# Windowed attention with one expert per sentence on one Trainium2 core: 64-column pooled sums for batch 0, and a new order of all steps

## The chip, the core and the metric

The kernel runs on one core of a Trainium2 chip. The core has TensorE (matrix products into PSUM), VectorE, ScalarE and GpSimd, and SyncE, which here issues stores. DMA engines move data between HBM and the core's memory, SBUF. GpSimd issues all loads, on one queue. The metric is the device time of one execution in microseconds (us), the median of several runs.

## The reference

The input is q, k and v for 8 batches ("sentences"), 8 heads, 576 positions and a head dimension of 64. Each head attends within a window of 32 positions on either side. The result, 576 x 512 for each batch, goes through one of 8 experts, chosen for the whole sentence from the mean over its positions:

```python
scores = scale * np.matmul(q, k.transpose(0, 1, 3, 2))
mask = np.abs(pos[:, None] - pos[None, :]) <= 32
attn = softmax(np.where(mask, scores, -1e9))          # per head
x = np.matmul(attn, v)                                # then B, S, H*D
pooled = x.mean(axis=1)                               # 8 x 512
logits = pooled @ w_gate                              # 8 x 8
e_idx = np.argmax(logits, axis=1)                     # one expert per batch
out[mask] = gate_w[mask, None, None] * (np.maximum(x[mask] @ w1[e], 0.0) @ w2[e])
```

The weights of an expert, 512 x 1024 and 1024 x 512, can be loaded only when the batch's pooled sums have chosen it.

## The kernel before

Each batch goes through the same steps, and each step has a short name with the batch number in it. For batch b:

- `ldqb`, `ldkb`, `ldvb` (L286, L314) load q, k and v, cast to 16 bits. `Tqb0`, `Tqb1` and so on (L300, L327) transpose them on VectorE.
- `Sb0` to `Sb2` (L417) are the score products on TensorE, `Xb..` (L440) the exponentials on ScalarE. In batches 0 and 1 a fill `ZSb.` (L397) first writes the window's mask into PSUM; in the others `Mb.` (L450) multiplies the mask in on VectorE.
- `Vb0`, `Vb1` (L347) turn v on TensorE, `Cb0`, `Cb1` (L360 on ScalarE, L362 on VectorE) copy it into the tile va, and `Db..` (L373 on ScalarE or VectorE, L375 on GpSimd) make its copies shifted by 64 positions, 64 x 528 numbers each.
- `Ab0` to `Ab2` (`Ab4` in batch 0) (L469) are the attention products, 28 + 28 + 16 of them in batch 1; `NAb.` (L541, L542) divides by the softmax sums on VectorE and so frees the PSUM pair.
- `Rb0`, `Rb1` (L571, L574) turn the result on TensorE, `CRb..` (L586 on VectorE, L588 on ScalarE in batch 0, L590 otherwise) copy it out as xT.
- `Lb` (L650, L655) makes the logits, `Gb` (L667, L668) finds the expert, `GNb` and `GXb` its exponentials, `W1b` and `W2b` (L695 and L719 for batch 0, L704 and L724 otherwise) load its weights. Batch 0's first weights come in three pieces, `W10`, `WB1` and `WB2`.
- `1b0` to `1b7` (L753) are the first expert products, eight matrix products each, `R1b.` their ReLU (L768, L770). `2b...` (L833, L796) are the second ones, `E2b...` scale and copy them out (L781, L784), and `O2b...` store them (L861, L814).

In batch 0 the pooled sums are made on TensorE itself, by the steps `pool0` to `pool4` (L616): each product has 64 columns of a unit of 128 rows of attention output as its stationary operand (the loaded weights), and as its moving operand one column, either ones (`pick`, parts 0 and 1, fp16) or the reciprocals of the softmax sums (`linv`, parts 2 to 4, fp32, which use the undivided output copied by `U02` to `U04`, L518 and L520, with the reciprocals from `I02` to `I04`, L507). Even and odd heads use the two column halves of the array. `pcopy` (L629) copies the 128 x 4 sums out of PSUM. In later batches the sums come with the copies CR, for nothing.

The order of the work is written out by hand in the string `ORDER`: one list of step names, with the engine behind a colon where there is a choice. `Plan.finish` (L109) goes through it and emits each step; each engine then runs its own steps strictly in that order, and waits where an operand isn't ready. GpSimd's list holds the loads, the shifted copies D, the pads and the broadcasts GB. Buffers are handed out in the same pass: PSUM is four pairs of banks, and a step that takes a pair gets the one that was freed first, so it waits for the step that freed it. In front of some TensorE steps `busy` (L234) issues products of a constant tile (`KEEP`), whose output is overwritten.

The order around the change, from the table: in the old order A10 comes after `100`, `wg` (the gate matrix of the later batches) ahead of `W10`, and `ldk4` ahead of `W12`.

Of the kernel before, what the change touches and what calls it, by code (L numbers as in the profile page):

```python
# [10 lines left out]
FP32 = mybir.dt.float32  # L11
# [13 lines left out]
P = 128  # L25
# [15 lines left out]
}  # L41

ORDER = """
ldq00 ldk00 ldv00 ldv01 ldk01 ldq01 cu0 ldk1 wg0 cp1 ldq1 cp0 ldv1 ldk2 ca cb Tq00 Tk00 ZS00 S00
X001 Tv00 V00 Tv01 X000 C00:DVE D001:ACT ZS01 V01 Tk01 D000:ACT Tq01 A00 C01:ACT D011:ACT D010:SW
wg ldq2 A01 cu1 NA00 NA01 S01 X011 X010 ZS02 S02 A03 A02 X021 X020 Tk10 Tk11 I03 U03:ACT A04 pool0
I02 U02:DVE I04 U04:ACT NA02 Tq10 Tq11 pool1 pool2 pool3 pool4 pcopy:ACT L0 G0 GN0 GX0 W10 NA03
Tv10 Tv11 ZS10 S10 X101 X100 ZS11 S11 WB1 WB2 V10 V11 Tk20 NA04 X110 Tk21 C10:ACT C11:DVE X111 R00
ldv2 CR000:ACT R01 CR001:ACT W20 CR010:DVE D101:SW CR011:DVE D100:SW ZS12 S12 100 Tq20 D110:SW Tq21
D111:SW X120 X121 A10 R100:ACT ldv3 NA10 A12 NA12 101 102 R101:ACT A11 R102:ACT S20 103 X201 NA11  # L50
R10 X200 R103:DVE Tv20 GW0 Tv21 R11 CR100 CR110 CR101 104 R104:ACT CR111 LP1 105 R105:ACT 106 ldk3
R106:DVE S21 X210 107 X211 R107:DVE L1 G1 GN1 W11 V20 C20:ACT V21 C21:ACT M21 M20 D201 GX1 D200
20000 Tv30 Tv31 20001 20010 S22 GW1 D210 X221 X220 20011 20100 D211 20101 M22 A20 A21 ldq3 20110
W21 20111 GB1 GB0 NA20 NA21 20t A22 E2000:ACT E2010:ACT V30 V31 NA22 E20t:ACT C30:ACT C31:DVE D310
D311 ldv4 Tk30 D300 Tk31 D301 R20 Tq30 CR200 R21 110 CR210 CR211 CR201 LP2 111 R110:ACT 112
R111:ACT 113 R113:ACT R112:DVE L2 G2 GN2 GX2 114 115 R114:ACT R115:ACT Tq31 S30 X301 X300 116 117
R116:ACT 21000 R117:ACT S31 X310 X311 M31 21001 21010 M30 Tv40 S32 X321 21011 21100 X320 Tv41
E2100:ACT 21101 21110 V40 21111 C40:ACT A30 M32 21t A31 ldq4 ldk4 E2110:ACT GW2 Tq40 A32 NA30 V41
E21t:ACT W12 W22 NA32 120 121 R120:ACT NA31 R30 R121:ACT C41:DVE D401 CR300 CR301 ldv5 O21t O2110
Tk40 D411 Tk41 D400 R31 Tq41 122 123 124 R122:ACT 125 CR310 CR311 R124:ACT R123:ACT ldq5 LP3 L3 G3  # L60
W13 GN3 D410 GB2 R125:ACT GX3 126 Tv50 S40 R126:ACT X401 127 22000 X400 S41 R127:DVE X411 X410
22001 22010 S42 X420 X421 Tv51 M40 Tq50 Tq51 ldk5 M41 22011 22100 E2200:DVE 22101 22110 22111 W23
A40 M42 O2000 E2210:ACT A42 22t NA40 NA42 E22t:ACT O22t ldv6 O2200 A41 130 NA41 V50 O2010 GW3 131
C50:ACT R130:DVE 132 R132:DVE R131:ACT Tk50 Tk51 R40 R41 D500 CR400 ldq6 CR410 CR411 133 134 135
CR401 LP4 L4 R134:ACT R135:ACT R133:DVE G4 GN4 GX4 136 R136:DVE S50 X500 W14 137 ldk6 23000 X501
R137:DVE W24 S51 X510 23001 Tv60 23010 Tv61 ldq7 GB3 X511 V51 23011 M50 C51:ACT GW4 GB4 23100 M51
E2300:ACT 23101 D510 Tq60 D501 S52 23110 X520 23111 X521 D511 23t M52 E2310:ACT E23t:DVE A50 NA50
O23t A51 A52 NA52 140 141 R140:ACT 142 R141:ACT NA51 R51 R50 R142:ACT Tq61 CR500 Tk60 Tk61 CR501
CR510 CR511 LP5 143 144 R144:ACT 145 R145:ACT R143:DVE V60 V61 C60:DVE C61:ACT D601 L5 G5 D611 GN5
GX5 146 R146:ACT 147 R147:DVE S60 X600 ldv7 X601 O2100 D610 O2300 24000 O20t D600 24001 W15 S61  # L70
24010 24011 X610 X611 Tq70 E2400:ACT Tq71 M61 S62 24100 X620 24101 ldk7 X621 24110 24111 M60
E2410:ACT Tv70 Tv71 A60 M62 24t NA60 E24t:ACT O24t A62 NA62 A61 V70 NA61 V71 C70:ACT 150 C71:ACT
R60 CR600 R150:DVE 151 R61 CR601 CR610 CR611 152 R152:ACT 153 154 R153:ACT Tk70 Tk71 R151:DVE W25
S70 D701 R154:ACT D710 GW5 LP6 X701 155 X700 R155:DVE L6 156 R156:ACT G6 GN6 D711 W16 GX6 M70 157
R157:ACT S71 W26 25000 GB5 25001 X711 X710 S72 X721 X720 M72 M71 D700 25010 25011 O2210 25100 25101
25110 25111 A70 E2510:ACT O2400 25t E2500:DVE NA70 A72 NA72 A71 NA71 160 161 R70 E25t:ACT R71
R160:DVE CR700 162 R161:DVE 163 CR710 CR701 CR711 R163:ACT 164 L7 R164:ACT G7 165 GN7 W17 GX7 166
R166:ACT 167 O2310 O2500 O2410 GW6 R165:DVE R167:ACT R162:DVE 26000 26001 26010 26011 GB6 26100
E2600:ACT O2600 W27 26101 GW7 26110 GB7 26111 E2610:DVE O2510 O2610 26t E26t:DVE O26t 170 R170:DVE
171 172 R172:ACT 173 174 175 R174:ACT R173:DVE R175:ACT 176 R171:DVE R176:ACT O25t 177 27000  # L80
R177:ACT 27001 27010 27011 E2700:DVE O2700 27100 27101 27110 27111 E2710:ACT E2711:ACT 27t O2710
E27t:DVE O2711 O27t
"""


# [46 lines left out]
def kernel(  # L132
# [126 lines left out]
    raw, qkv, E_of, va_of, xs_of, xT_of, h_of, w_of, bank_of = {}, {}, {}, {}, {}, {}, {}, {}, {}  # L259
# [14 lines left out]
    def add_batch(b):  # L274
# [514 lines left out]
        for at, T in enumerate(order2):  # L789
# [56 lines left out]
            for e0, e1 in pieces:  # L846
# [7 lines left out]
                n = 512 * (e1 - e0)  # L854
# [43 lines left out]
```

## Time and profile before

| | us |
|---|---|
| median of 3 runs | 199.75 (199.63 to 199.96) |
| profiled execution | 199.34 |
| its span, first to last instruction | 197.6 |
| TensorE busy | 187.2 (95%) |
| VectorE busy | 135.0 (68%) |
| ScalarE busy | 116.1 (59%) |
| GpSimd busy | 49.8 (25%) |
| mean granted TensorE clock | 0.989 of full |

The profile is of one execution. Times in its rows are us from the start of the span. PE is TensorE, PEld its loading of weights, DVE is VectorE, ACT ScalarE, POOL GpSimd. A row names the line of the kernel (L616), what is written and read, shapes, and the number of instructions (x48). The chain of waits is followed back from the last instruction: what it shows at a time is what the end waited for at that time. Matrix products are pipelined and their ends modelled, so a busy TensorE is not one at its peak. A granted clock of 1.00 is 2.4 GHz, 0.50 is 1.2 GHz.

### The profile page before, as it was taken

To read this page: it belongs to the slowest core of one execution; us is meant where nothing else is said; L and a number is where in the kernel's file an instruction comes from. 1 tells how busy PE (TensorE), PEld (TensorE's weight loads), DVE (VectorE), ACT (ScalarE), POOL (GpSimd) and SP (SyncE) were. 2 spreads that over 40 slices of the span, in tenths; PEclk is the share of its full clock that TensorE was granted. 3 is DMA by queue.
4 is the path that set the end of the run, shared out by engine and by line. 5 is a ranking of instruction groups with operands and counts; after the bars stand their busy time and mean duration, and the time that the engine had idled before them with its cause. 6 is when DMAs were issued, how large, how long until landed. Compare 5 with 4: busy or idle time off the path is not lost.

```text
span 197.6 us, 6965 instructions
## 1 busy us (share of the span) xinstructions
PE 187.2 (95%) x3068; PEld 137.0 (69%) x3068; DVE 135.0 (68%) x237; ACT 116.1 (59%) x200; POOL 49.8 (25%) x108
## 2 busy tenths in 40 slices
PE   6878988999999999999999999999999999999992
PEld 2356666874799559964997579946996499659741
DVE  6799998878794399789786859679853682314120
ACT  2177475885597664973486657776896238221511
POOL 7804193008063002260025500350304000300000
PEclk9999889999999999999999999999999999999999
DMA  4999999999999999999999999999998994699624
GB/s 77 194 214 214 213 159 208 207 219 167 213 226 180 215 215 215 292 216 211 224 202 279 241 222 212 298 180 207 219 261 214 216 202 194 90 219 223 268 94 149
DMA packets 12733, 40.84 MB, mean 207 GB/s; under 512 B 1280, under 2 KB 3872, under 8 KB 11808
## 3 DMA queue, kind: packets, MB, share of 16 engines
q0 software_dynamic: 8976, 30.97, 82.7%
q1 hardware_dynamic: 3648, 9.37, 12.3%
q8 instruction: 24, 0.39, 0.7%
q10 hardware_dynamic: 80, 0.07, 0.1%
q14 instruction: 5, 0.04, 0.1%
HBM read 61.90 MB, written 9.44 MB: 361 GB/s over the span
## 4 chain that ended last, share of the span: by engine, by line
PE 70%; DMA 16%; DVE 7%; issue 2%; POOL 2%; POOLq 1%; ACT 0%; DVEq 0%
PE pair L753 28%; PE pair L833 25%; DMA w<-in_moe_w_dram 10%; DMA raw<-in_k_dram 5%; PE pair L417 4%; PE pair L469 3%; PE pair L796 3%; PE pair L347 3%; PE pair L571 3%; DVE kT L327 2%; POOL raw L286 2%; DVE qT L327 1%; DVE xs L542 1%; POOLq L698 1%; DVE va L362 0%
## 5 line engine op out<-in xcount | busy, mean ns | idle before, releaser
L753 PE MATMUL pair<-xT,w 128*128 128x288 f16 x512 | 68.5, 288 | 0.8 <-issue 0.4
L753 PEld LDWEIGHTS <-w 128*128 128x128 f16 x512 | 59.9, 139 | 2.9 <-DMA w<-in_moe_w_dram 0.7
L833 PE MATMUL pair<-w,hT 128*128 128x512 f16 x256 | 58.8, 380 | 0.0
L440 ACT ACTIVATE E<-pair 128x768 f16<-128x768 f32 (+2 forms) x48 | 36.3, 809 | 18.0 <-PE pair L417 18.0
L833 PEld LDWEIGHTS <-hT 128*128 128x128 f16 x256 | 23.9, 98 | 25.9
L768 ACT ACTIVATE hT<-pair 128x576 f16<-128x576 f32 x42 | 27.0, 654 | 21.4 <-PE pair L753 20.9
L375 POOL COPY va<-va 64x528 f32<-64x528 f32 x29 | 17.9, 624 | 60.6 <-ACT va L360 37.7
L450 DVE TENSOR_TENSOR E<-E,mask 128x1536 f16<-128x1536 f16 x18 | 16.7, 947 | 14.8 <-ACT E L440 14.8
L781 ACT ACTIVATE osb<-pair,gwb 128x1024 f32<-128x1024 f32 (+1 forms) x13 | 13.6, 1049 | 20.5 <-PE pair L833 10.5
L542 DVE TENSOR_TENSOR xs<-pair,linv 128x896 f16<-128x896 f32 (+1 forms) x23 | 23.2, 1008 | 0.8
L770 DVE TENSOR_SCALAR hT<-pair 128x576 f16<-128x576 f32 x22 | 16.3, 752 | 10.2 <-PE pair L753 10.1
L590 ACT ACTIVATE xT<-pair 128x576 f16<-128x576 f16 x28 | 17.9, 652 | 4.2 <-PE pair L574 4.2
L704 POOL DMA_DIRECT2D w<-in_moe_w_dram x7 | 5.0, 710 | 48.5 <-issue 23.6
L360 ACT COPY va<-pair 128x1280 f16<-128x1280 f16 x11 | 13.3, 1225 | 6.6 <-PE pair L347 5.5
L327 DVE STREAM_TRANSPOSE kT<-raw 128x576 f32<-128x576 f32 x14 | 16.5, 1250 | 0.5 <-DMA raw<-in_k_dram 0.5
L327 DVE STREAM_TRANSPOSE vT<-raw 128x576 f32<-128x576 f32 x14 | 16.1, 1209 | 0.8 <-DMA raw<-in_v_dram 0.6
L327 DVE STREAM_TRANSPOSE qT<-raw 128x576 f32<-128x576 f32 x14 | 16.4, 1214 | 0.0
L417 PEld LDWEIGHTS <-kT 32*128 32x128 bf16 x1152 | 11.0, 94 | 7.8 <-issue 6.9
L469 PEld LDWEIGHTS <-E 128*64 128x64 f16 x576 | 11.1, 111 | 5.6 <-issue 3.9
L784 DVE TENSOR_SCALAR osb<-pair,gwb 128x1024 f32<-128x1024 f32 x4 | 5.1, 1276 | 13.3 <-PE pair L833 13.3
L469 PE MATMUL pair<-va,E 128*64 128x65 f16 x576 | 12.6, 196 | 1.5 <-ACT va L360 0.7
L417 PE MATMUL pair<-qT,kT 32*128 32x64 bf16 x1152 | 13.5, 191 | 0.3 <-POOL vT L226 0.2
(87 smaller groups left out, 163.6 us busy)
## 6 DMA issues: line engine op xcount, KB each, us to landing
w<-in_moe_w_dram POOLq DMA_DIRECT2D x15, 1024.0 KB, 13.7
out_dram<-osb SPq DMA_DIRECT2D x15, 512.0 KB, 10.2
raw<-in_k_dram POOLq DMA_DIRECT2D x7, 576.0 KB, 12.1
raw<-in_q_dram POOLq DMA_DIRECT2D x7, 576.0 KB, 10.3
raw<-in_v_dram POOLq DMA_DIRECT2D x7, 576.0 KB, 10.4
out_dram<-osm SPq DMA_DIRECT2D x15, 64.0 KB, 7.7
raw<-in_q_dram POOLq DMA_DIRECT2D x2, 288.0 KB, 6.4
raw<-in_k_dram POOLq DMA_DIRECT2D x2, 288.0 KB, 6.3
```

The costliest lines, as they stand in the source:

```text
L327: nc.vector.transpose(dst[:, t0:t1], src[:, t0:t1].rearrange("p t (g r) -> p t g r", g=2),)
L375: (nc.gpsimd if op.eng == "SW" else nc.vector).tensor_copy(dst, src)
L417: nc.tensor.matmul(bk[a // 2][:, a % 2, 64 * c : 64 * c + 64], kt[rows, g, par, 64 * i : 64 * i + 128], qt[rows, g, par, 64 * i : 64 * i + ...
L440: nc.scalar.activation(ev, bank_of[sn][m][:, :, 0:w].rearrange("p a (g c) -> p a g c", g=n_g), ACTF.Exp, bias=0.0, scale=0.125,)
L450: nc.vector.tensor_tensor(ev, ev, mask.rearrange("p n c -> p (n c)").unsqueeze(1).broadcast_to([P, 8, 192]), ALU.mult)
L469: nc.tensor.matmul(pair[64 * half : 64 * half + 64, m // row, 65 * (m % row) : 65 * (m % row) + 65], ev[:, g, a, 64 * i : 64 * i + 64], va ...
L542: nc.vector.tensor_tensor(xs_of[b][:, D * n0 : D * n1].rearrange("p (n m x two) -> p n m two x", n=nb, x=32, two=2), hv[:, :, :, 0:64].rea ...
L590: nc.scalar.activation(dst, src, ACTF.Copy, accum_out=tiny("pooled", [P, 4], FP32, b)[:, 2 * blk + e : 2 * blk + e + 1],)
L753: nc.tensor.matmul(pair[:, c, 0:288], w1v[:, kt], xT_of[b][:, kt, 288 * c : 288 * c + 288], start=(kt == 0), stop=(kt == 3),)
L768: nc.scalar.activation(dst, src, ACTF.Relu)
L770: nc.vector.tensor_single_scalar(dst, src, 0.0, ALU.max)
L833: nc.tensor.matmul(bank_of[(on, e)], hv.rearrange("p (m two) -> p two m", two=2)[:, e], w2v(ft), start=(ft == 0), stop=(ft == NFT - 1),)
```

## The change

The moving operand of each pooled product becomes 64 columns, all the same: the one column is read with a stride of zero. So each product writes 64 equal output columns, a head pair's block at 0, 64, 128 or 192 of the bank, and `pcopy` keeps the first of each 64. In part 4 the two loops are exchanged, so that successive products take the two column halves in turn there too. And the whole string `ORDER` is new; it has the same steps, but their order and some of the engines differ from the first line to the last.

```diff
-                    for n in range(4 if part == 4 else 8):
-                        for half in range(2 if part == 4 else 1):
+                    for half in range(2 if part == 4 else 1):
+                        for n in range(4 if part == 4 else 8):
                             h = 4 * half + n if part == 4 else 2 * part + n % 2
...
                             nc.tensor.matmul(
-                                bank_of["pool"][64 * (h % 2) : 64 * (h % 2) + 64, 0, h // 2 : h // 2 + 1],
-                                x, weigh, start=part == 0 and n < 2, stop=part == 4,
+                                bank_of["pool"][64 * (h % 2) : 64 * (h % 2) + 64, 0, 64 * (h // 2) : 64 * (h // 2) + 64],
+                                x, weigh.broadcast_to([P, 64]), start=part == 0 and n < 2, stop=part == 4,
                                 tile_position=(0, 64 * (h % 2)), skip_group_check=True,
...
-                dst, src = tiny("pooled", [P, 4], FP32, b), bank_of.pop("pool")[:, 0, 0:4]
+                dst, src = tiny("pooled", [P, 4], FP32, b), bank_of.pop("pool")[:, 0, 0:256:64]
```

The beginning of the order, and the places further on that the prediction speaks of:

```diff
-ldq00 ldk00 ldv00 ldv01 ldk01 ldq01 cu0 ldk1 wg0 cp1 ldq1 cp0 ldv1 ldk2 ca cb Tq00 Tk00 ZS00 S00
-X001 Tv00 V00 Tv01 X000 C00:DVE D001:ACT ZS01 V01 Tk01 D000:ACT Tq01 A00 C01:ACT D011:ACT D010:SW
-wg ldq2 A01 cu1 NA00 NA01 S01 X011 X010 ZS02 S02 A03 A02 X021 X020 Tk10 Tk11 I03 U03:ACT A04 pool0
-I02 U02:DVE I04 U04:ACT NA02 Tq10 Tq11 pool1 pool2 pool3 pool4 pcopy:ACT L0 G0 GN0 GX0 W10 NA03
-Tv10 Tv11 ZS10 S10 X101 X100 ZS11 S11 WB1 WB2 V10 V11 Tk20 NA04 X110 Tk21 C10:ACT C11:DVE X111 R00
-ldv2 CR000:ACT R01 CR001:ACT W20 CR010:DVE D101:SW CR011:DVE D100:SW ZS12 S12 100 Tq20 D110:SW Tq21
-D111:SW X120 X121 A10 R100:ACT ldv3 NA10 A12 NA12 101 102 R101:ACT A11 R102:ACT S20 103 X201 NA11
...
-R111:ACT 113 R113:ACT R112:DVE L2 G2 GN2 GX2 114 115 R114:ACT R115:ACT Tq31 S30 X301 X300 116 117
...
-E2100:ACT 21101 21110 V40 21111 C40:ACT A30 M32 21t A31 ldq4 ldk4 E2110:ACT GW2 Tq40 A32 NA30 V41
-E21t:ACT W12 W22 NA32 120 121 R120:ACT NA31 R30 R121:ACT C41:DVE D401 CR300 CR301 ldv5 O21t O2110
...
-CR510 CR511 LP5 143 144 R144:ACT 145 R145:ACT R143:DVE V60 V61 C60:DVE C61:ACT D601 L5 G5 D611 GN5
-GX5 146 R146:ACT 147 R147:DVE S60 X600 ldv7 X601 O2100 D610 O2300 24000 O20t D600 24001 W15 S61
...
+ldq00 ldk00 ldv00 ldv01 ldk01 ldq01 cu0 cp1 ldk1 ldq1 cp0 cu1 wg0 ca cb ZS00 Tq00 Tk00 S00 X001
+X000 Tv00 Tv01 V00 C00:DVE ZS01 D000:ACT V01 D001:ACT C01:ACT Tk01 A00 D010:ACT D011:SW ldv1 A01
+Tq01 ldq2 NA00 NA01 S01 ZS02 X010 ldk2 S02 Tk10 A02 X011 Tk11 I02 A03 X021 I03 X020 U03:DVE pool0
+A04 U02:ACT I04 pool1 pool2 Tq10 pool3 Tq11 U04:ACT pool4 NA02 pcopy:ACT L0 G0 ZS10 W10 WB1 WB2 S10
+GN0 GX0 ZS11 Tv10 Tv11 X101 S11 X100 V10 wg V11 NA04 X111 NA03 R00 X110 R01 C10:DVE D100:DVE
+D101:DVE C11:ACT D110:SW ZS12 D111:SW CR000:ACT CR001:ACT CR010:ACT CR011:ACT S12 X121 Tq20 X120
+A10 100 Tq21 101 ldv2 W20 Tk20 Tk21 R100:ACT R101:ACT NA10 ldv3 A12 NA12 102 R102:ACT A11 S20 NA11
...
+D300 CR210 CR211 LP2 Tq31 113 114 R113:ACT R114:ACT 115 L2 R112:ACT R115:ACT 116 G2 W12 ldk4 S30
+GN2 GX2 R116:ACT ldv5 X301 X300 D301 117 R117:ACT 21000 S31 Tv40 Tv41 21001 X311 21010 X310 S32
...
+R50 Tk61 143 144 R51 O2310 CR500 CR501 R144:ACT R143:ACT 145 V61 R145:DVE CR510 CR511 146 147 D601
+ldv7 C61:ACT D610 LP5 L5 G5 W15 GN5 Tq70 R146:ACT Tq71 24000 GW4 R147:ACT S60 X600 X601 M60 GX5
```

## Rows read from the trace of the kernel before

**Rows 1.** The page: DMA share in 40 slices, in tenths; DMA totals.
```profile
DMA  4999999999999999999999999999998994699624
...
DMA packets 12733, 40.84 MB, mean 207 GB/s; under 512 B 1280, under 2 KB 3872, under 8 KB 11808
```

**Rows 2.** The chain of waits: start, duration in us, what it was.
```profile
23.96 6.00 DMA w<-in_moe_w_dram
...
30.01 1.16 PE pair L753 x8
31.17 0.82 PE pair L469 x44
...
33.93 0.36 issue
...
34.57 0.56 PE pair L469 x28
...
35.62 1.09 PE pair L753 x8
...
61.64 14.38 DMA w<-in_moe_w_dram
...
76.06 2.18 PE pair L753 x16
...
177.76 7.99 PE pair L753 x64
...
192.66 1.01 PE pair L796 x16
```

**Rows 3.** Windows: length, TensorE busy (instructions), granted clock, DMA share, GB/s.
```profile
22.00:23.00 1.00, 0.92 (x51) 0.88 1.08 221
...
26.00:27.00 1.00, 1.00 (x20) 0.92 1.06 150
...
30.00:34.00 4.00, 3.92 (x67) 1.00 1.21 211
34.00:36.00 2.00, 1.71 (x81) 1.00 1.01 200
...
75.00:80.00 5.00, 4.91 (x70) 1.00 1.02 207
```

**Rows 4.** DMA issues in 15.8 to 15.9: size, us from issue to landing.
```profile
raw<-in_q_dram POOLq DMA_DIRECT2D x1, 576.0 KB, 12.0
```

**Rows 5.** Timeline of TensorE: start, us, line, operation, count.
```profile
19.18 1.59 PE L616 MATMUL pair<-linv,osb 128*64 128x1 f32 x48 [0.40 <-DVE osb L520]
...
21.30 0.82 PE L397 MATMUL pair<-nmask,id_f 128*128 128x384 f16 x4
...
22.69 1.43 PE L397 MATMUL pair<-nmask,id_f 128*128 128x384 f16 x4
...
25.30 1.69 PE L347 MATMUL pair<-id_f,vT 128*128 128x128 f16 x20 [0.42 <-DVE vT L327]
```

**Rows 6.** Timeline of VectorE; in brackets idle time before, and what ended it.
```profile
22.01 0.14 DVE L667 MAX8 top<-pair 1x8 f32<-1x8 f32 x1
...
28.59 0.90 DVE L586 COPY xT<-pair 128x576 f16<-128x576 f16 x2 [0.28 <-PE pair L574]
...
31.77 0.24 DVE L541 RECIPROCAL linv<-pair 128x14 f32<-128x14 f32 x1
...
33.33 0.73 DVE L542 TENSOR_TENSOR xs<-pair,linv 128x512 f16<-128x512 f32 x1
```

**Rows 7.** Timeline of GpSimd and ScalarE.
```profile
15.84 0.56 POOL L314 DMA_DIRECT2D raw<-in_q_dram  x1
...
26.47 1.23 ACT L360 COPY va<-pair 128x1280 f16<-128x1280 f16 x1 [0.74 <-PE pair L347]
...
27.82 2.52 POOL L375 COPY va<-va 64x528 f32<-64x528 f32 x4 [0.34 <-ACT va L360]
...
28.29 1.19 ACT L588 COPY xT<-pair 128x576 f16<-128x576 f16 x2
```

More of the change, by code (lines that the diff above doesn't have):

```diff
@@ L49 @@
-ldv2 CR000:ACT R01 CR001:ACT W20 CR010:DVE D101:SW CR011:DVE D100:SW ZS12 S12 100 Tq20 D110:SW Tq21
-D111:SW X120 X121 A10 R100:ACT ldv3 NA10 A12 NA12 101 102 R101:ACT A11 R102:ACT S20 103 X201 NA11
[L51 to L54, printed above, removed]
@@ L55 @@
-D311 ldv4 Tk30 D300 Tk31 D301 R20 Tq30 CR200 R21 110 CR210 CR211 CR201 LP2 111 R110:ACT 112
-R111:ACT 113 R113:ACT R112:DVE L2 G2 GN2 GX2 114 115 R114:ACT R115:ACT Tq31 S30 X301 X300 116 117
-R116:ACT 21000 R117:ACT S31 X310 X311 M31 21001 21010 M30 Tv40 S32 X321 21011 21100 X320 Tv41
-E2100:ACT 21101 21110 V40 21111 C40:ACT A30 M32 21t A31 ldq4 ldk4 E2110:ACT GW2 Tq40 A32 NA30 V41
-E21t:ACT W12 W22 NA32 120 121 R120:ACT NA31 R30 R121:ACT C41:DVE D401 CR300 CR301 ldv5 O21t O2110
-Tk40 D411 Tk41 D400 R31 Tq41 122 123 124 R122:ACT 125 CR310 CR311 R124:ACT R123:ACT ldq5 LP3 L3 G3
@@ L61 @@
[L61 to L66, printed above, removed]
@@ L67 @@
-E2300:ACT 23101 D510 Tq60 D501 S52 23110 X520 23111 X521 D511 23t M52 E2310:ACT E23t:DVE A50 NA50
-O23t A51 A52 NA52 140 141 R140:ACT 142 R141:ACT NA51 R51 R50 R142:ACT Tq61 CR500 Tk60 Tk61 CR501
-CR510 CR511 LP5 143 144 R144:ACT 145 R145:ACT R143:DVE V60 V61 C60:DVE C61:ACT D601 L5 G5 D611 GN5
-GX5 146 R146:ACT 147 R147:DVE S60 X600 ldv7 X601 O2100 D610 O2300 24000 O20t D600 24001 W15 S61
-24010 24011 X610 X611 Tq70 E2400:ACT Tq71 M61 S62 24100 X620 24101 ldk7 X621 24110 24111 M60
-E2410:ACT Tv70 Tv71 A60 M62 24t NA60 E24t:ACT O24t A62 NA62 A61 V70 NA61 V71 C70:ACT 150 C71:ACT
@@ L73 @@
[L73 to L82, printed above, removed]
+ldq00 ldk00 ldv00 ldv01 ldk01 ldq01 cu0 cp1 ldk1 ldq1 cp0 cu1 wg0 ca cb ZS00 Tq00 Tk00 S00 X001
+X000 Tv00 Tv01 V00 C00:DVE ZS01 D000:ACT V01 D001:ACT C01:ACT Tk01 A00 D010:ACT D011:SW ldv1 A01
@@ new lines @@
+Tq01 ldq2 NA00 NA01 S01 ZS02 X010 ldk2 S02 Tk10 A02 X011 Tk11 I02 A03 X021 I03 X020 U03:DVE pool0
[3 more added lines that the diff above has]
+A10 100 Tq21 101 ldv2 W20 Tk20 Tk21 R100:ACT R101:ACT NA10 ldv3 A12 NA12 102 R102:ACT A11 S20 NA11
+103 X201 R103:DVE X200 R10 ldk3 Tv20 R11 CR100 GW0 GB0 CR110 CR111 CR101 104 LP1 R104:ACT 105 Tv21
@@ new lines @@
+R105:ACT 106 S21 R106:DVE 107 L1 G1 GN1 W11 X210 V20 X211 R107:ACT GX1 V21 C20:DVE M21 M20 C21:ACT
+D211 S22 D210 X220 X221 D200 20000 20001 20010 20011 20100 20101 20110 20111 Tv30 Tv31 D201
+E2000:DVE ldq3 M22 A20 E2010:ACT W21 NA20 A22 20t A21 E20t:ACT V30 NA22 C30:ACT V31 NA21 ldv4
+C31:ACT D310 110 R110:ACT R20 D311 CR200 Tk30 GW1 Tq30 CR201 ldq4 GB1 111 R111:DVE 112 Tk31 R21
+D300 CR210 CR211 LP2 Tq31 113 114 R113:ACT R114:ACT 115 L2 R112:ACT R115:ACT 116 G2 W12 ldk4 S30
+GN2 GX2 R116:ACT ldv5 X301 X300 D301 117 R117:ACT 21000 S31 Tv40 Tv41 21001 X311 21010 X310 S32
@@ new lines @@
+X321 M31 X320 21011 E2100:ACT 21100 21101 W22 M30 M32 Tq40 21110 21111 E2110:ACT Tq41 A30 21t A31
+NA30 E21t:DVE A32 V40 120 NA32 V41 C40:ACT R120:ACT GW2 GB2 NA31 121 Tk40 R121:ACT C41:DVE R30 R31
+Tk41 D401 CR300 122 CR310 CR311 CR301 ldq5 123 124 125 LP3 R122:ACT R123:DVE S40 R124:ACT R125:ACT
+X400 O21t 126 R126:ACT O2000 X401 L3 127 22000 G3 GN3 GX3 W13 S41 R127:DVE 22001 X411 22010 M40
+Tv50 Tv51 D411 D400 X410 O2010 D410 ldk5 S42 M41 X421 W23 X420 M42 22011 22100 E2200:DVE 22101
+22110 22111 ldv6 E2210:ACT O2200 A40 O2210 A42 NA40 22t E22t:ACT O22t NA42 A41 V50 V51 C50:ACT 130
@@ new lines @@
+NA41 R40 C51:DVE D510 D500 D511 D501 Tq50 GW3 R41 131 Tk50 R130:ACT 132 ldk6 CR400 Tk51 CR401 133
+CR410 CR411 R132:ACT 134 LP4 L4 R133:ACT 135 Tq51 R131:ACT R134:ACT R135:ACT G4 W14 136 S50 ldq6
+GN4 GX4 R136:DVE GB3 W24 X501 X500 137 R137:ACT 23000 Tv60 Tv61 S51 X510 23001 X511 23010 23011
+23100 E2300:ACT M51 M50 S52 X521 X520 23101 23110 V60 23111 E2310:ACT M52 A50 C60:DVE D600 23t NA50
+E23t:DVE O23t O2300 A51 NA51 A52 NA52 ldq7 140 R140:ACT Tk60 141 142 R142:ACT Tq60 R141:DVE Tq61
+R50 Tk61 143 144 R51 O2310 CR500 CR501 R144:ACT R143:ACT 145 V61 R145:DVE CR510 CR511 146 147 D601
@@ new lines @@
+ldv7 C61:ACT D610 LP5 L5 G5 W15 GN5 Tq70 R146:ACT Tq71 24000 GW4 R147:ACT S60 X600 X601 M60 GX5
+24001 24010 S61 X611 X610 ldk7 M61 24011 Tv70 W25 Tv71 24100 D611 S62 GB4 X620 X621 M62 24101 24110
+24111 E2400:ACT E2410:ACT A60 NA60 24t E24t:ACT O24t O20t A62 A61 O2400 V70 NA62 C70:ACT V71 NA61
+C71:ACT O2100 150 R150:DVE R60 D711 CR600 151 CR601 R151:ACT Tk70 152 R61 Tk71 R152:DVE CR610 CR611
+153 R153:ACT 154 R154:ACT LP6 S70 X701 X700 155 D700 GW5 GB5 R155:ACT D701 L6 G6 GN6 GX6 W16 156
+157 R156:DVE S71 X711 W26 X710 R157:DVE 25000 D710 25001 25010 25011 25100 S72 X721 X720 E2500:DVE
@@ new lines @@
+M71 25101 25110 25111 M70 E2510:ACT M72 A70 NA70 A72 25t E25t:ACT O25t NA72 A71 NA71 160 161
+R160:DVE R70 R71 162 R161:DVE CR700 CR701 163 CR710 CR711 R163:ACT 164 R164:ACT L7 R162:ACT 165
+R165:ACT GW6 GB6 166 167 26000 G7 W17 R167:ACT R166:DVE 26001 26010 26011 O2410 E2600:DVE GN7 26100
+GX7 26101 26110 26111 O2110 E2610:DVE O2600 W27 O2610 26t GW7 E26t:ACT GB7 O26t O2500 O2510 170
+R170:DVE 171 R171:DVE 172 R172:ACT 173 174 R174:DVE R173:ACT 175 176 177 R176:ACT 27000 R177:ACT
+R175:DVE 27001 27010 27011 E2700:DVE 27100 27101 27110 27111 O2700 27t E2710:DVE E2711:ACT O2710
@@ L83 @@
+O2711 E27t:DVE O27t
 """
```

## The prediction

> **What bounds the kernel now.** The page comes first [rows 1]: the DMA row is full from the second slice until near the end, at a mean of 207 GB/s. Then the chain of waits [rows 2]: the first weights of batch 0 are issued at 23.96 and land 6.00 later, at 29.96, and the first expert product (the step `100`, 8 matrix products) starts at 30.01. From there to the last product, 192.66 + 1.01 = 193.67, the chain is almost only TensorE. The windows [rows 3] say how much idle time is left in that stretch: 0.08 + 0.29 in 30 to 36 (a hole of 0.36 before 34.29, charged to "issue", that is, to nothing the profile shows), 0.09 in 75 to 80; nearly all else is work. So the end can come earlier in three ways: `100` starts earlier, work that now follows `100` is done before it, or one of those holes closes.
>
> What sets 29.96 is not the choice of the expert. The last 576 KB load ahead of these weights, q of batch 2, was issued at 15.84 and took 12.0, so it landed at 27.8 [rows 4, 7]; the weights stand behind it in one queue of busy DMA engines. Issued somewhat later, they would still land then.
>
> **The clock.** The granted clock falls from 1.00 to 0.50 at about 22.9 and is back before 26.3 [rows 3]: with three slices at 0.50 between those shown, (0.12 + 3 x 0.50 + 0.08) / 0.50 = 3.4 us at half speed, 1.2 instead of 2.4 GHz. Just before came the one-column products and the logits. The price is visible: four 384-column products take 0.82 at 21.30 and 1.43 at 22.69 [rows 5]. But this stretch lies ahead of 29.96, under the weights' landing, and what it slows, batch 1's scores and transposes, waits for VectorE anyway: VectorE has its first hole after the choice at 22.01 only at 28.59 [rows 6].
>
> **The change part by part.**
> 1. *Pooled products, 64 columns for 1.* 16 fp16 products, and 24 fp32 products that the trace records as 48, in 1.59 us [rows 5]. No row shows fp32 with 64 columns. A gain is excluded, since every weight load stays. Lower bound: nothing, if the columns pass under the loads: in a stream 288 columns take 7.99 / 64 = 0.125 [rows 2], so 64 take 0.028 and 48 records 1.33, less than the 1.59 they have. Upper bound: none of it overlaps, +1.33. I take 0, the nearer row being the stream, and because the new loop alternates the column halves in part 4 too. Cover: the products end at 20.77, and the fill behind the logits starts at 21.30, but VectorE comes to the choice only at 22.01 [rows 5, 6], behind q of batch 1; in the new order Tq10, Tq11 and NA02 still stand ahead of it. So about 0.7 is free; each us beyond delays VectorE, and batch 1 with it.
>
> [...] The trace shows two records for each product and nothing inside them. [...]
>
> 2. *The clock stretch.* If it goes, 1.43 - 0.82 = 0.61 on the fill and as much again on scores and transposes come free, all before 29.96: 0 on the path. If it stays, batch 1's value transposes take 1.69 [rows 5], not about 1.25, C11 comes 0.5 later, and the four copies CR0, all on ScalarE now at 0.60 each [rows 7], end near 30.1: `100` 0 to 0.25 late. I take 0.
>
> 3. *A10 ahead of `100`.* In the old order A10 (28 of the 44 attention products that take 0.82 at 31.17 [rows 2]) comes after `100`, in the new one before. It issues no DMA. It waits for va with its shifted halves and for a PSUM pair freed by CR001. Tv10 and Tv11 now come straight behind the choice, so both are through near 24.6 and V11 near 26.0; C11 (1.23 [rows 7]) ends by 27.3. D100 and D101 go to VectorE; D110 and D111 stay on GpSimd, two copies of 2.52 / 4 = 0.63 [rows 7], done by 28.6; CR001 by 28.5, CR011 by 29.7. `100` is queued behind A10 but waits for 29.9 in any case, so A10 has some 0.9 to spare. -28/44 x 0.82 = -0.52.
>
> 4. *What follows on VectorE.* S20 needs PSUM pairs that NA10 and NA12 free. Between the choice and NA10 (31.77), VectorE's new list is the old one in another order, except that the two copies CR010 and CR011 (0.90, with a hole of 0.28 before them [rows 6]) make way for D100 and D101. By the nearest rows one of these takes between 0.42 (0.45 scaled by 528 to 576 columns) and 0.63 (the same copy on GpSimd); I take 0.6. So NA10 starts between 31.77 - 0.34 and 31.77 + 0.08; NA12 ends 2.29 later, as before (34.06), at 33.7 to 34.15. TensorE is there at 29.9 + 3 x 1.09 for `100` to `102` (as at 35.62 [rows 2]) + 16/44 x 0.82 for A12 + 0.56 for A11 = 34.0. The two meet, 1.1 before the old S20 (34.57 + 0.56 = 35.13, after A11). So the hole of 0.36 may close: between 0 and -0.36, half: -0.18.
>
> 5. *Loads.* ldv1 and ldk2 go behind the copy D011 on GpSimd's queue, next to where q2 was issued (15.84). The queue was then 12.0 deep, so the engines don't run dry, and the same eight tensors stand ahead of the first weights. The gate matrix `wg` (16 KB) goes behind batch 0's W1: 0 to -0.2 by its place, -0.05 by its size. At batch 2 the old order has k4 ahead of W12, which landed at 61.64 + 14.38 = 76.02; TensorE began on it at 76.06 [rows 2], so there a gain would have been lost. The new order has k4 behind: 576 KB at 207 GB/s, 2.8 us earlier. That keeps the gain; of its hole of 0.09 I count half, -0.05.
>
> 6. *The rest of the order.* After the start the same TensorE steps are interleaved differently. Eight expert products behind another kind of step take 1.09 to 1.16, 7.99 / 8 = 1.00 in the stream [rows 2], so a break costs 0.1 to 0.16; counted in both orders, 71 breaks between tile shapes become 70: 0. The last evictions and stores keep their form: 0.
>
> Sum: -0.52 - 0.18 - 0.05 - 0.05 = -0.80. The profiled execution has a span of 197.6 and a time of 199.34, with 1.74 around the span; it becomes 196.8 and 198.54. It is 0.41 below the median of the three runs, so for the median I forecast 199.75 - 0.80 = 198.95.
>
> **Rivals.**
> - *Weights hold TensorE back.* For: the DMA row is full, W12 landed 0.04 before its use, and L5, which chooses batch 5's expert, moves behind `146` and `147`, 2 x 1.09 later [rows 2]. Against: stores start later, and k4 and va copies get out of the way. Then 0.6 of the 0.8 is given back: 199.55.
> - *More than the sum.* The holes of 0.36 and 0.09 close, and `wg` is worth its 0.2: -0.52 - 0.36 - 0.09 - 0.2 = -1.17, 198.6; VectorE's gain of 0.34 can push that to 198.4.
> - *The pool grows past its cover.* 1.33 - 0.7 = 0.63 late on VectorE, NA12 ends at 34.35 to 34.8, and S20 gains 0.5 of its 0.9: 199.35.
> - *Slower: half-clock time behind 30 us.* If the narrow products aren't its cause, or the new order is thinner elsewhere (TensorE idles about 1 us before `100`), 3.4 us at half speed fall on full work. Price 3.4 / 2 = 1.7 on 198.95: 200.65. It decides once over 1.6 us of it lie behind `100`. For: the clock fell although TensorE was recorded 0.92 busy. Against: all windows shown behind 30 have 1.00 [rows 3].
> - *The change doesn't do what it says*, the clock falls all the same and in the same place: by step 2 it costs 0 to 0.25 and stays inside the forecast.
>
> **How the numbers follow.** Forecast 0.52 (its own range 198.6 to 199.4), weights 0.16, more 0.12, pool 0.08, slower 0.12. A measurement of this kernel tells about 0.2%, 0.4 us, from no change: the border of faster is 199.35. Faster: 0.93 of the forecast, all of "more", half of "pool", 0.64. Slower: the last rival and a little of the weights', 0.14. Same: the remaining 0.22. The range reaches from 198.2, below "more", to 200.0: it leaves out the slower rival and little else.
>
> **What would show it.** `100` at 29.8 to 30.0 with A10's 28 products before it; later than 30.1, and step 2, 3 or 5 is wrong. S20 near 34.2. The granted clock between 22 and 27 shows whether the columns matter to it, and the start of `100` whether that matters to the time. fp32 pooled products over 2.2 us refute step 1. `120` should not wait for W12. The forecast is wrong if TensorE has holes of over 0.2 in front of expert products after 40 us, or half speed after 30.

## The result and the profile after

The changed kernel took 201.69 us, the median of 9 runs (201.06 to 202.58); the kernel before took 199.96 in the runs beside it (9 runs, 199.34 to 200.94). The ratio is 1.0067, with an interval of 1.0045 to 1.0089: slower by 0.9 to 1.8 us. (A ratio here is taken over the fast runs and is not the quotient of the medians, which would be 1.0087.) Forecast were 198.95 and a range that ended at 200.0. Neither the forecast nor any rival has the cause.

The profiled execution of the changed kernel took 201.89, with a span of 200.2: 2.55 and 2.6 more than in the profile of before. That is more than the 1.73 between the medians, since the profile of before is of the quickest of its nine runs. The page of the changed kernel: the granted clock and the DMA share in 40 slices, the queue of instructions (packets, MB, share of the engines' time), and the cost of the first expert line (busy, mean ns, idle before):

```profile
PEclk9999999999999999999999999999999999999998
DMA  4999999998999799999999999999996985699823
...
q8 instruction: 24, 0.39, 0.7%
...
L753 PE MATMUL pair<-xT,w 128*128 128x288 f16 x512 | 68.9, 287 | 1.5 <-issue 1.5
```

The DMA row is as full as before [rows 1], and the half clock of before [rows 3] is gone from the clock's row. A product of L753 takes 287 ns, before 288. New are idle times of TensorE in front of expert products, put down to "issue". The chain of waits shows them in their places (start, us, what), and [rows 2] answer to it:

```profile
27.11 0.68 issue
...
29.59 0.56 PE pair L469 x28
30.15 2.07 PE pair L753 x16
32.22 0.37 PE pair L469 x16
32.59 0.96 PE pair L753 x7
33.56 1.53 issue
35.09 0.28 PE pair L753
35.37 0.56 PE pair L469 x28
35.93 0.48 PE pair L417 x46
...
44.56 0.48 PE pair L417 x46
45.05 0.76 PE pair L833 x3
45.80 1.40 issue
47.21 6.42 PE pair L833 x29
...
194.90 1.01 PE pair L796 x16
```

The whole difference of the two profiles can be read from this chain. `100` starts at 30.15, 0.14 later than before, with A10 done ahead of it (29.59), which saves 0.52 behind it. It no longer waits for the weights: their first piece, issued at 23.81, landed 5.2 later, at 29.0. It waits for TensorE, which stood from 27.11 to 27.80 for nothing that the chain names ("issue"). The hole of 0.36 has become 1.53: +1.17. Before the fourth product of `20000`, where TensorE had no hole in the old order, there is one of 1.40. The sum is 0.14 - 0.52 + 1.17 + 1.40 = +2.19. The last product ends at 195.91, before at 193.67: +2.24. Everything else moved the end by 0.05. This sum is that of two single executions, and the two holes don't stand on the same footing: the experiments below show what the second one costs, but the first is of different size from one execution to the next.

In windows of the changed kernel (length, TensorE busy with its products, granted clock, DMA share, GB/s), as in [rows 3]:

```profile
30.00:34.00 4.00, 3.56 (x49) 1.00 1.20 212
34.00:36.00 2.00, 0.91 (x47) 1.00 1.02 199
...
75.00:80.00 5.00, 5.00 (x124) 1.00 1.08 220
```

**What the holes are.** The page of each kernel has a DMA queue "q8 instruction" with 24 packets and 0.39 MB, 16 KB each. TensorE has 3068 loads of weights and 3068 products in the page, and (3068 + 3068) / 24 = 255.7. That suggests that these packets are TensorE's program, in blocks of 256 instructions. To see whether it is so, count the products and the loads between the holes of the changed kernel (windows of all engines: length; busy and count of PE, PEld, DVE, ACT, POOL; clock, DMA share, GB/s):

```profile
27.75:35.05 7.30, 5.76 (x128) 4.28 (x128) 6.09 (x8) 4.42 (x7) 3.17 (x6) 1.00 1.19 194
35.05:41.58 6.53, 6.46 (x128) 5.02 (x128) 4.09 (x9) 5.50 (x13) 0.26 (x1) 1.00 1.10 211
41.58:47.15 5.57, 4.22 (x130) 3.10 (x130) 4.97 (x10) 5.14 (x9) 1.87 (x2) 1.00 0.93 175
```

From 27.80, where an idle time ends, to the hole before 35.09 there are 128 + 128 = 256 instructions, one block; from there to the hole before 47.21 there are two blocks (four instructions under way at the edge at 41.58 are counted on both sides of it). Each hole lies where a block ends, and a packet of program is under way ahead of each. DMA packets that start in 32.5 to 32.8, and in 44.5 to 45.0:

```profile
q8 instruction: 1, 0.02, 20.2%
...
q8 instruction: 1, 0.02, 11.2%
```

By their own records they move from 32.65 to 33.62 and from 44.89 to 45.78, and TensorE goes on 1.4 to 1.5 us after each landing. Even the weights' loads stop, each time one ahead of the products (8 loads of L753 from 32.52 to 7 products, 4 of L833 from 44.98 to 3). TensorE's weight loads in 33 to 36 and in 45 to 48:

```profile
35.30 0.52 PEld L469 LDWEIGHTS <-E 128*64 128x64 f16 x28 [1.93 <-issue]
...
47.21 0.74 PEld L833 LDWEIGHTS <-hT 128*128 128x128 f16 x4 [1.69 <-issue]
```

So the theory (call it *instruction supply*): TensorE gets its program one block ahead. When it begins a block, the next one is called for; its packet starts later, behind the data in the full DMA engines (3.0 to 4.9 us in the first 50 us of the two kernels), moves for 0.9 to 1.0, and can be used 1.2 to 1.5 after that: 5.6 to 7.3 us in all at the four places where one of the two kernels stood for it behind 25 us. A block that is used up sooner ends in a hole. How soon depends on what is in it: an expert step is 16 instructions in 1.09 us, a score step (`S22`) 96 in 0.5, an attention step (A11) 56 in 0.56. The call itself is in no trace; the packets and the holes are. The idle time of 0.68 that ends at 27.80 is such a place too: its packet landed at 26.56, 1.24 before.

The kernel before has the same ends of blocks. Its windows (TensorE) from one to the next:

```profile
27.80:34.25 6.45, 5.75 (x128) 1.00 1.18 189
34.25:40.68 6.43, 6.39 (x131) 1.00 1.10 211
40.68:46.47 5.79, 5.79 (x131) 1.00 1.06 201
```

Its hole of 0.36 [rows 2] was the end of a block too. The third block has work for 5.79 us, and the next packet comes in time (by its record 43.71 to 44.60). In the new order S22 stands ahead of `20000`, 96 instructions that take 0.5; the same block is issued from 41.58 to 45.42, in 3.84 us, and the next packet starts no sooner after its beginning, 3.31 against 3.05.

### The profile page after: what moved, and what is told of

The parts are those of the page before. It is cut to its first block, busy times and chain, and to the rows that moved or that the text cites. A ratio compares the mean times of both kernels' runs of the same rounds, so it can differ in the third digit from the quotient of the medians.

```text
span 200.2 us, 6981 instructions
## 1 busy us (share of the span) xinstructions
PE 186.5 (93%) x3068; PEld 136.2 (68%) x3068; DVE 137.6 (69%) x238; ACT 114.1 (57%) x201; POOL 49.4 (25%) x106
## 4 chain that ended last, share of the span: by engine, by line
PE 84%; DVE 4%; DMA 3%; issue 3%; ACT 3%; POOL 1%; DVEq 0%; ACTq 0%; POOLq 0%
PE pair L753 33%; PE pair L833 28%; PE pair L469 5%; PE pair L417 5%; PE pair L347 4%; PE pair L796 4%; PE pair L571 4%; DMA raw<-in_v_dram 3%; ACT va L360 1%; DVE vT L327 1%; DVE qT L327 1%; POOL raw L286 1%; ACT E L440 1%; ACT va L373 1%; DVE vT L300 1%
## 5 line engine op out<-in xcount | busy, mean ns | idle before, releaser
L753 PE MATMUL pair<-xT,w 128*128 128x288 f16 x512 | 68.9, 287 | 1.5 <-issue 1.5
L753 PEld LDWEIGHTS <-w 128*128 128x128 f16 x512 | 59.8, 139 | 2.1 <-issue 0.2
L833 PE MATMUL pair<-w,hT 128*128 128x512 f16 x256 | 58.7, 380 | 1.4 <-issue 1.4
L833 PEld LDWEIGHTS <-hT 128*128 128x128 f16 x256 | 23.9, 98 | 27.9 <-issue 1.7
L768 ACT ACTIVATE hT<-pair 128x576 f16<-128x576 f32 x45 | 28.6, 656 | 17.7 <-PE pair L753 17.4
L781 ACT ACTIVATE osb<-pair,gwb 128x1024 f32<-128x1024 f32 (+1 forms) x10 | 10.7, 1074 | 21.9 <-PE pair L833 17.5
L770 DVE TENSOR_SCALAR hT<-pair 128x576 f16<-128x576 f32 x19 | 14.3, 759 | 8.0 <-PE pair L753 7.1
L784 DVE TENSOR_SCALAR osb<-pair,gwb 128x1024 f32<-128x1024 f32 (+1 forms) x7 | 8.5, 1208 | 15.7 <-PE pair L833 13.7
L360 ACT COPY va<-pair 128x1280 f16<-128x1280 f16 x10 | 12.1, 1229 | 4.4 <-PE pair L347 4.4
L731 POOL PARTITION_BROADCAST gwb<-gw x8 | 2.1, 259 | 43.0 <-DVE gw L688 32.9
```

Source lines behind the costliest of these rows:

```text
L753: nc.tensor.matmul(pair[:, c, 0:288], w1v[:, kt], xT_of[b][:, kt, 288 * c : 288 * c + 288], start=(kt == 0), stop=(kt == 3),)
L768: nc.scalar.activation(dst, src, ACTF.Relu)
L770: nc.vector.tensor_single_scalar(dst, src, 0.0, ALU.max)
L833: nc.tensor.matmul(bank_of[(on, e)], hv.rearrange("p (m two) -> p two m", two=2)[:, e], w2v(ft), start=(ft == 0), stop=(ft == NFT - 1),)
```

## The experiments

All ratios are to the kernel before, run beside each kernel on the same chip. Holes and starts are those of one profiled execution.

**Undo the second hole.** S22 and its exponentials go back behind `20010`, nothing else:

```diff
-D211 S22 D210 X220 X221 D200 20000 20001 20010 20011 20100 20101 20110 20111 Tv30 Tv31 D201
+D211 D210 D200 20000 20001 20010 S22 X220 X221 20011 20100 20101 20110 20111 Tv30 Tv31 D201
```

> The changed kernel with one edit of its order: S22 (48 small score products, 96 instructions) with X220 and X221 goes back behind `20010`, where the old order has it. Theory F (TensorE runs out of instructions: they come in blocks of 16 KB over the DMA engines, and a block full of small products is used up before the next is there): the hole of 1.40 us before the fourth product of `20000` falls below 0.4, the hole of 1.53 inside `102` stays, and the time is 1.0 to 1.7 us under the changed kernel's, a ratio to the kernel before of 0.999 to 1.003. Rival W (the new order brings weights or VectorE's and ScalarE's results too late, and the profile only fails to name them): the hole stays where it is, since S22 is no operand of `20000`, and the time stays within 0.4 us of the changed kernel's.

Measured: 199.73, ratio 0.9992 (0.996 to 1.0024). Its windows of TensorE from block end to block end, and its chain's only "issue" over 0.1 behind 30:

```profile
27.90:34.90 7.00, 5.76 (x128) 1.00 1.19 199
34.90:41.47 6.57, 6.51 (x135) 1.00 1.12 216
41.47:47.26 5.79, 5.79 (x135) 1.00 0.90 161
```
```profile
33.67 1.25 issue
```

The third block again holds work for 5.79 us, and its hole is gone; the first hole stays. Moving one step of 0.5 us by a few places brings back the whole loss, 0.75% or 1.5 us (0.7 to 2.3 by the two intervals), and the hole had 1.40. The first hole, 1.25 here, is still there in a kernel that is as fast as the one before.

**Each half of the change alone.** The 64 columns in the old order, and the new order with one column:

> The 64-column pooled products alone, in the old order. Theory F: the granted clock stays at 1.00 from 22 to 27 us, but the time is that of the kernel before, ratio 0.998 to 1.002, since that stretch lies under the landing of the first weights and the number of instructions is the same; the hole inside `102` is there as before (0.3 to 0.8). Rival C (the wider products or the clock cost the time): slower by most of the 0.67%, ratio 1.004 to 1.007.

> The new order alone, with one-column pooled products. Theory F: the time of the changed kernel, ratio to before 1.005 to 1.009, both holes of over 1 us are there, and the half-speed stretch comes back near 23 to 26 us without costing more than 0.3. Rival C: like the kernel before, ratio within 0.002.

Columns alone: 200.01, 1.0000 (0.9966 to 1.0034). Order alone: 201.22, 1.0052 (1.0021 to 1.0083), with both holes. The loss is the order's. One thing was not as expected: with the columns alone, in the old order, the hole inside `102` was 1.01 and not 0.3 to 0.8. It is in that profile's chain:

```profile
35.11 1.01 issue
```

There the block was begun at 28.56, its packet started 5.05 after that, and TensorE went on at 36.12, 1.49 after the landing. So the old order can have a first hole of over 1 us too, and the 0.36 of the kernel before against the 1.53 of the changed one does not show that the order made it larger. The second hole is another matter: the changed kernel and the order alone have it, with S22 ahead of `20000`; the kernel before, the columns alone and the run with S22 put back do not. Windows 20 to 23 and 23 to 27, of the columns alone and of the order alone:

```profile
20.00:23.00 3.00, 2.59 (x59) 1.00 1.08 216
23.00:27.00 4.00, 2.94 (x120) 1.00 0.97 183
```
```profile
20.00:23.00 3.00, 2.39 (x80) 0.93 1.04 210
23.00:27.00 4.00, 4.00 (x95) 0.63 1.08 199
```
And the holes of the order alone in its chain:
```profile
34.16 0.98 issue
...
45.85 1.14 issue
```

In 23 to 27 the clock is 1.00 with the columns alone and 0.63 with the order alone, which has one column (0.60 in the kernel before), and no difference in the time is seen (1.0000 for the columns alone).

**A10 behind `100` again**, in the changed kernel:

```diff
-A10 100 Tq21 101 ldv2 W20
+100 A10 Tq21 101 ldv2 W20
```

> The changed kernel with A10 (28 small products) back behind `100`, all else as changed. Theory F: both steps stand before the same end of a block, so the hole inside `102` ends when the next block of instructions is there, wherever A10 is: it becomes shorter by A10's 0.4 to 0.6 us, the step after it starts within 0.3 of the same time (35.1), and the time stays within 0.4 us of the changed kernel's, ratio to before 1.004 to 1.008. My prediction's step 3 (A10 ahead of `100` is worth its 0.52): 0.5 us slower than the changed kernel, ratio 1.008 to 1.010, and the step after `102` 0.5 later.

Measured: 201.38, 1.0075 (1.004 to 1.0111), beside 1.0067 for the changed kernel. A10's place is worth nothing that can be seen, but this does not decide between the two expectations: 0.52 us is 0.26%, less than either interval is wide. Nor does the profile. Its clock is at 0.64 in 30 to 33, TensorE comes to the end of the block only at 36.0, 2.4 after the packet landed, and so there is no hole inside `102`; the step after it starts at 36.30 and not near 35.1, and the hole at `20000` is 0.47. That A10 and `100` lie in the same block, so that `102` waits for the next one whichever of them is first, stays an argument.

**More instructions, no more work.** In the kernel before, 32 products of one column, 64 instructions with their loads, into an unused bank, ahead of batch 0's logits:

```diff
+            for i in range(32 if b == 0 else 0):
+                nc.tensor.matmul(
+                    op.got["ps"][0][64 * (i % 2) : 64 * (i % 2) + 64, 1, 0:1],
+                    fill_in[:, 0:64], fill_in[:, 0:1], start=True, stop=True, ...
```

> The kernel before with 32 useless one-column products (64 instructions) put in front of batch 0's logits, where TensorE has idle time; they go to the free half of the logits' PSUM pair. Theory F: every later step stands 64 instructions deeper, so the blocks end at earlier work: the hole that was inside `102` moves to A12 or `101` and grows, and the time rises by 1.0 to 3.0 us, ratio 1.005 to 1.015. Rival W, or no effect of the number of instructions: the 32 products take about 0.5 us in a stretch that has more cover than that, so the time rises by 0 to 0.4 us, ratio 1.000 to 1.002.

Measured: 203.78, 1.0189 (1.0116 to 1.0262): +3.8 us, more than I expected. The chain:

```profile
21.65 0.82 issue
27.25 1.24 issue
...
34.18 1.05 issue
40.56 0.86 issue
```

Four holes where there was one of note, in front of other steps than before: the ends of the blocks have moved, 64 instructions earlier in the work. The holes add up to 3.97, and 0.36 were there. The products' own time is not told apart from this, and a late choice costs here too, so the size is no proof; the new places are. They can be counted. Number TensorE's weight loads and products in order of time, from 0. In the profiles of the kernel before, the changed kernel and the ten runs there are 27 stretches of over 0.3 us between 20 and 60, at least one in each profile, in which neither a load nor a product runs and behind which the next number is 187 (once 188) above a multiple of 256, in this kernel as in the others. Each of them ends 1.2 to 1.5 us after a program packet landed.

**Fewer instructions.** In the changed kernel 16 of the 24 fp32 pooled products are left out, 64 instructions:

```diff
                             if part > 1 and n > 1:
+                                continue
```

> The changed kernel without 16 of its 24 fp32 pooled products (64 TensorE instructions): part of batch 0's pooled sums is missing, so batch 0 may take another expert of the same size. Theory F, the reverse of the padded kernel: every block ends 64 instructions later in the work, so TensorE has more work before each hole: 0.6 to 2.0 us under the changed kernel, ratio to before 0.996 to 1.003. Rival W: the products lie in a stretch where VectorE is awaited anyway, nothing changes, ratio 1.004 to 1.008.

Measured: 200.33, 1.0033 (1.0 to 1.0067), just above what was expected. The hole at `20000` is gone and the first is smaller, 0.51 in the chain, where the changed kernel has 1.53:

```profile
34.45 0.51 issue
```

It points the right way, but the interval overlaps that of the changed kernel, and the chain of its profile runs over other engines up to that hole.

**Where the wait for a packet comes from.** The loads of v and k of batch 3 go behind the weights of batch 1, so that the DMA engines run dry around 42:

```diff
-... NA10 ldv3 A12 ... R10 ldk3 Tv20 ... GN1 W11 X210
+... NA10 A12 ... R10 Tv20 ... GN1 W11 ldv3 ldk3 X210
```

> The changed kernel with the loads ldv3 and ldk3 moved behind W11 on GpSimd, so that the load queue runs empty for some us when batch 0's W2 has landed (about 42.5 to 47). TensorE's order is untouched. Theory F with its second half (the instruction block waits behind the loads in the DMA engines): the block asked for at 41.7 starts to move in under 1.5 us instead of 3.3, and the hole of 1.40 inside `20000` falls below 0.5. Rival F' (a block takes its 6 us whatever else moves): the hole stays at 1.2 to 1.7. The whole time is no test here, as v and k of batch 3 come later: between 1.5 us faster and 1 us slower than the changed kernel, ratio 0.998 to 1.012.

Its windows (TensorE; the fifth number is the DMA share), its chain, and the packet that starts in 42 to 43:

```profile
36.00:44.00 8.00, 7.96 (x170) 1.00 0.74 140
44.00:48.00 4.00, 4.00 (x74) 1.00 0.40 37
```
```profile
34.19 0.98 issue
...
45.91 10.10 DMA raw<-in_v_dram
```
```profile
q8 instruction: 1, 0.02, 7.8%
```

The same block of TensorE's program is begun at 41.66 here and at 41.58 in the changed kernel. The next packet starts 0.5 later here (42.13 by its record), where full engines made it wait 3.3, and S22's hole is gone with S22 in its place: TensorE is busy for 4.00 of the 4.00 us from 44. The first hole, with full engines, stays (0.98). This is the sharpest evidence for the mechanism. The time, 209.59 (1.0497, 1.0461 to 1.0533), is worth nothing as a version: the chain then waits 10.10 for v of batch 3. The cost of the late load was far outside what I expected.

**Spread the small steps.** Three orders of the stretch between A10 and `20111`. All put five expert steps, with 80 instructions in 5 us, ahead of A12 and A11, and S22 behind the first second-layer products; the second has S20 straight behind A11 and S21 ahead of V20, the third S21 behind `20000`.

```diff
-A10 100 Tq21 101 ldv2 W20 ... A12 NA12 102 R102:ACT A11 S20 NA11 103 X201 R103:DVE
+A10 100 Tq21 101 ldv2 W20 Tk20 Tk21 R100:ACT 102 R101:ACT NA10 ldv3 103 R102:ACT 104 R103:DVE A12
+R104:ACT A11 NA12 S20 NA11 105 X201 X200 R105:ACT 106 R106:ACT Tv20 R10 R11 ...
```

> The changed kernel with the steps between A10 and `20111` in another order: `100` to `104` first, then A12 and A11, then `105`, `106`, R10, R11, `107`, V20, V21, and S20, S21 and S22 spread out between the second products. Each block of 256 TensorE instructions then holds 6 us of work or more. Theory F: no hole of over 0.5 us between 30 and 50 us, `20000` starts at 42.5 to 43.5 (in the changed kernel 45.05), and the time falls below both kernels: 198.2 to 199.3 where the kernel before has 199.9, ratio 0.991 to 0.997. Rival W (what counts is that batch 2's scores and batch 1's attention come early): A20 to A22, R20 and R21 wait for the later exponentials, and the time is no better than the kernel before, ratio 1.000 to 1.010.

> The changed kernel with its order between A10 and 20111 rearranged a second time: five expert products ahead of the small products A12, A11 and S20, which spreads the small ones as in the first spread, but S20 comes straight behind A11, S21, V20 and V21 behind 107, and S22 behind 20011. Theory (TensorE runs out of instructions where a block of small products is used up early): the hole in 33 to 36 falls from 1.5 us to under 0.3 and that in 45 to 48 from 1.4 to under 0.3, as in the first spread, and because the work now lies so that VectorE and ScalarE are ready earlier, 20000 starts at 43.0 to 43.6 with S20 and S21 done (44.2 with both done in the kernel with S22 put back): ratio to before 0.993 to 0.999. Rival (the holes only hide waits for data: weights' third piece, PSUM pairs, transposes of v): the holes go and as much waiting for data comes, 20000 at 44.0 to 44.4, ratio 0.999 to 1.003.

> The same rearrangement, but S21 behind 20000 and X201, X200 behind R105. Theory: the instruction holes are as small as in the other kernel; S21 behind 20000 takes one PSUM pair less ahead of it, so 20000 starts 0.5 earlier and ends up level: ratio to before 0.993 to 1.000. Rival: 20000 waits for the pair that C20 or C21 frees, as in the first spread (0.33), ratio 0.999 to 1.004.

Measured: 200.75, 1.0025 (0.9981 to 1.0068); 200.40, 0.9997 (0.9964 to 1.0031); 200.89, 1.0019 (0.9983 to 1.0055). The holes at the ends of blocks behind 30 us are gone in all three, and the gain isn't there: all missed. TensorE's timeline of the second, from the third step on:

```profile
30.72 5.07 PE L753 MATMUL pair<-xT,w 128*128 128x288 f16 x40
...
38.55 1.14 PE L753 MATMUL pair<-xT,w 128*128 128x288 f16 x8 [0.17 <-DVE xs L542]
...
42.33 0.54 PE L417 MATMUL pair<-qT,kT 32*128 32x64 bf16 x46 [0.51 <-ACT xT L590]
...
44.59 3.61 PE L833 MATMUL pair<-w,hT 128*128 128x512 f16 x16 [0.23 <-DVE va L362]
```

No hole here is put down to "issue", but `20000` starts at 44.59, not at 43.0 to 43.6. Of that, 0.6 is the first step's start at 30.72 (30.09 in the changed kernel's timeline), and 0.17 + 0.51 + 0.23 are waits for VectorE's and ScalarE's results, whose copies now stand behind each other. In the first of the three it is the weights' third piece (0.43) and the transposes of v (0.31) as well. The rival of these runs, that waits for data take the holes' place, holds. So in these three orders the first hole was not free time: what was closed of it, the stretch mostly lost to the data that is due next. None of these orders, nor S22 put back, beats the kernel before.

## Why the prediction was wrong

The step that failed is the sixth, "The rest of the order ... 0". I counted breaks between tile shapes and took it that the order of the same TensorE steps costs nothing else. It cost the second hole, +1.40 in the profile; with S22 alone put back, the ratio went from 1.0067 to 0.9992. Even then the rest of the sum is not seen: 199.75 - 0.80 would be a ratio of 0.996, which is the edge of that run's interval. The prediction had named the sign of it, a hole of over 0.2 in front of an expert product after 40 us.

The second failure is in step 4. I had the hole of 0.36 on the table, called it "nothing the profile shows", and let VectorE's earlier start close half of it. VectorE did what I said: NA10 starts at 31.69 (foreseen 31.43 to 31.85), and NA12 ends at 33.19 + 0.72 = 33.91 (foreseen 33.7 to 34.15). VectorE, new kernel, against [rows 6]:

```profile
31.69 0.18 DVE L541 RECIPROCAL linv<-pair 128x14 f32<-128x14 f32 x1
...
33.19 0.72 DVE L542 TENSOR_TENSOR xs<-pair,linv 128x512 f16<-128x512 f32 x1
```

But S20 began at 35.93 and not near 34.2, since TensorE stood from 33.56 to 35.09 in the middle of `102` for want of instructions. An idle time that ends with no event of another engine was not a small VectorE wait to be shaved, but a wait for the program, which I did not look for; the row "q8 instruction" stood on the page.

Point by point:

1. *Pooled products, 0.* Right. The 48 fp32 records take 1.62, with one column 1.59 [rows 5]; of the upper bound, +1.33, only 0.03 came. TensorE's timeline:

```profile
19.10 1.62 PE L616 MATMUL pair<-linv,osb 128*64 128x64 f32 x48 [0.46 <-ACT osb L518]
```

2. *The clock stretch, 0 on the path.* No run speaks against it: columns alone 1.0000 (0.9966 to 1.0034), with the stretch gone.
3. *A10, -0.52.* The move happened as written (29.59, ahead of `100` at 30.15), and the engines' times were as foreseen (C11 ends at 27.11, CR011 at 29.68). But the 0.9 that A10 had to spare was not there: TensorE stood until 27.80 for its program, so `100` came at 30.15 behind A10, past the 30.1 that the prediction gave as a sign of error, though its weights were there at 29.0. What was gained behind `100` went into the hole at the end of the same block in this profile: the earlier TensorE reaches the end of a block whose successor comes no earlier, the longer it waits. The run with A10 moved back is too coarse to show it.
4. *The hole, -0.18.* Wrong, +1.17 in this pair of profiles. By the records TensorE reached the end of the block 0.37 earlier than before (33.27 against 33.64), which only lengthens the hole, and the next block could be used 0.80 later (35.09 against 34.29), as its packet started 4.85 after the block before it was begun and not 4.09. Why it waited longer is open, and it need not be the order: with the columns alone, in the old order, the packet waited 5.05 and the hole was 1.01. What is shown is that an earlier VectorE did not close it.
5. *Loads, -0.10.* No hole is left before `120` (window 75 to 80 is full, 5.00), so the wait of 0.09 went. Too small to be seen in the time.
6. *The rest, 0.* Wrong, +1.40, as above.

Of the rivals, the half clock behind 30 us came nearest, 200.65, for a wrong reason: the clock is 1.00 from 30 to 36. Weights that hold TensorE back did not decide the changed kernel, whose chain has no DMA behind 30; they show only in the first spread order.

The traces agree with a lead of one block, not of more: the 27 idle stretches counted above end 1.2 to 1.5 us after the packet that had landed last. The third block of the kernel before, with work for 5.79 us, ended 1.9 after the next packet had landed (44.60), with no hole; 1.53 and 1.40 are what TensorE stood in the changed kernel.

## What to carry to other kernels

Count instructions as well as time: where TensorE's stretch of 256 instructions held many small ones and the DMA engines were full, it ran dry (S22's block was issued in 3.84 us, and TensorE stood 1.40 behind it), and the profile says "issue" where its loads stopped with its products (1.69 and 1.40 us there). Read such a hole from the count of instructions between holes and from the packets of the instruction queue, and mix small steps with large ones so that every block lasts as long as a packet takes (5.6 to 7.3 us at the holes of these two kernels). But look at what data is due behind the hole before counting it as a gain, and at a second profile before putting a hole's size down to a change: the same hole was 0.36 and 1.01 in the same order.

## What was not expected of the hardware

- A program packet of 16 KB started 3.0 to 4.9 us after TensorE began the block before it, with full DMA engines, in the first 50 us of the two kernels, and 0.5 with idle ones in the run with the later loads. The wait is not fixed: between 50 and 80 us it was 1.0 to 3.3 in the two kernels.
- In all twelve profiles the idle stretches of over 0.3 us between 20 and 60 at a block's start ended 1.2 to 1.5 us after the packet's landing.
- 64 columns in place of one cost fp32 products 0.03 of 1.6 us.
- The granted clock fell to 0.50 around 23 to 27 with one-column products, in the old order and in the new (0.60 and 0.63 as means over 23 to 27). With 64 columns it stayed at 1.00 in 20 to 36 in the profiles of the changed kernel, of the columns alone, of S22 put back and of the first two spread orders, but not in all: with A10 moved back it was 0.64 and in the third spread order 0.51 in 30 to 33, with pooled products left out 0.62 and with the later loads 0.54 in 20 to 23. What else lowers it stays open; each of these stretches is of one execution. In the kernel before, at 1.00, 512-column products of L833 in a row started 0.216 us apart and 288-column ones of L753 0.1225, so 224 columns more took 0.093: 2.4 a nanosecond; at 0.50 its 384-column fills started 0.320 apart and 128-column transposes 0.107: 1.2 a nanosecond. Over all runs the mean granted clock was 0.989 to 1.000 with the columns alone (10 runs), 0.977 to 0.991 with the new order alone (10 runs), and 0.979 to 0.991 in the kernel before beside them (25 runs).
